# Memory attention and channel mixer in one kernel: the maxima of phi move from GpSimd to VectorE and small transfers, and the attention products go over whole tiles

## The chip, the cores and the metric

The kernel runs on one core of one Trainium2 chip. The metric is the device time of one execution in microseconds (us), as the median of several executions. TensorE multiplies matrices, VectorE, ScalarE and GpSimd work on tiles elementwise, and SyncE issues most transfers between device memory (DRAM) and the on-chip memory. Each engine, and SyncE's queue of transfers, works through its own list strictly in order.

## The reference

For each of 8 batches and 8 heads (576 positions, head size 64, 32 memory slots):

```python
a = phi - np.max(phi, axis=2, keepdims=True)          # over the positions, per memory slot
a = np.exp(a); a = a / (np.sum(a, axis=2, keepdims=True) + 1e-09)
k_m = np.einsum('bhsm,bhsd->bhmd', a, k)              # 32 keys and 32 values per head
v_m = np.einsum('bhsm,bhsd->bhmd', a, v)
scores = scale * np.matmul(q, k_m.transpose(0, 1, 3, 2))
attn = softmax(scores)                                # over the 32 slots
x = np.matmul(attn, v_m)                              # heads joined: (8, 576, 512)
h = np.maximum(x.T @ w_tok1, 0) @ w_tok2              # mixing over positions
u = x + h.T
out = u + np.maximum(u @ w_ch1, 0) @ w_ch2            # mixing over channels
```

## The kernel before, in words

A **quad** is one batch and one half of its heads (four heads); quad (4,1) is batch 4, second half. A quad's steps on TensorE are: `get_kv` (tile `kvp`, sums of keys and values over the positions), a small turn of `T` into `kb`, `scores` (tiles `sp`), `A` (tile `Ap`, the attention weights times `w_tok1`), `R` (tile `Rp`) and `u` (four tiles `u`, each one half of the channels by one half of the positions). Between `scores` and `A` lie the softmax on VectorE and ScalarE, a trip of its result through DRAM (`rows_out`, `rows_in`) that turns the layout, and a split of it into a high and a low part (`nat_high` on ScalarE, `nat_low` on GpSimd). Most products are made of such high and low parts, three products for one.

The results `u` are cut into chunks of 512 positions. The channel layers of a chunk (tiles `cp` and `acc`, 128x512 products) are the bulk of TensorE's work. The program has three parts in time. In the first, batches 0 and 1 are done between loads and conversions of the weights. In the second, the twelve quads from batch 2 on run, and the channel layers of chunks 1 and 2 fill TensorE between their steps. In the third, the remaining chunks are done in pairs by a scheme with seven products in place of eight; no quad is left there.

In the second part a planner sets the order of the work. Each step has an engine, an assumed duration in us, the steps it follows, the buffers ("rooms") it takes or uses, and a due time that serves as its rank; quad n is due `PERIOD` later than quad n-1. The planner plays the list through once and writes each engine's instructions in the order that results; on the chip nothing is reordered.

The maximum that is taken from phi before the exponential only has to be the same over the positions of one head and slot. `phi_max` (line 644, by `_red`, line 446) reduces on VectorE over the five blocks of positions within a partition, and `phi_all` (line 630) then takes the maximum over the 128 partitions with a GpSimd call. `phi_sub` (line 633, GpSimd) subtracts it, `phi_only_exp` (line 455, ScalarE) follows, and then `get_kv` can start. The planner's entries for these, as they stand in the second part:

```python
z = do(-17, "DVE", 1.35, qd.phi_max, z, take=[m], use=[phi_room])
z = do(-16, "POOL", 0.9, qd.phi_all, z, take=[r], use=[m])
z = do(-14, *PHI_SUB(qd), z, use=[phi_room, r], port=True)
e = do(-12, "ACT", 0.8, qd.phi_only_exp, z, use=[phi_room])
```

The weights of attention for `u` are kept in two tiles per quad, each with the high part of 64 rows in one half of the partitions and their low part in the other (`a_high`, `a_low`); `v_pair` (line 708) copies the high values twice to match. The tile S of the softmax has one room.

Of the kernel before, what the change touches and what calls it, by code (L numbers as in the profile page):

```python
# [20 lines left out]
P = 128  # L21
# [7 lines left out]
def kernel(  # L29
# [4 lines left out]
    phi: bass.AP,  # L34
    w_tok1: bass.AP,
# [58 lines left out]
    warm = wp.tile([P, 1], F32, tag="ps", name="warm", bufs=2)  # L94
# [5 lines left out]
    c1 = {}  # L100
# [240 lines left out]
    class Sums:  # L341
# [9 lines left out]
        def words(s):  # L351
            s.w = [sb.tile([P, 2, 256], F32, tag="al", name=f"w{j}{s.p}", bufs=2) for j in range(2)]
            for j, w in enumerate(s.w):
                h, l = (t[:, 2 * j : 2 * j + 2] for t in c1[s.p])
                nc.vector.tensor_tensor(out=w, in0=f32(h), in1=f32(l), op=ALU.add)

        def sum(s):
            t = wide(F32R, f"sums{s.p}").rearrange("p a n -> p (a n)")
            s.t = t
            s.v = v = t.rearrange("p (o x m) -> p o x m", o=4, x=2)  # L360

            def at(o):
                return f32(v[:, o, 1]).rearrange("p (a n) -> p a n", a=2)

            (w11, w21), (w12, w22) = ((w[:, :, :P], w[:, :, P:]) for w in s.w)
# [60 lines left out]
    class Quad:  # L426
# [17 lines left out]
        def _red(s, op):  # L444
            m = sb.tile([P, 4 * M], F32, tag="pr", name="pr" + s.n, bufs=3)
            nc.vector.tensor_reduce(
                out=m.rearrange("p (i m) -> p i m", i=4),
                in_=s.pt.rearrange("p i j m -> p i m j"),
                axis=AX.X,
                op=op,  # L450
            )
            return m

# [15 lines left out]
        def scales(s):  # L469
            s.ms = wp.tile([P, 6], F32, tag="ms", name="ms" + s.n, bufs=1)  # L470
            sm = wp.tile([P, 1], F32, tag="ps", name="ps" + s.n, bufs=2)
# [5 lines left out]
        def double_T(s):  # L477

            s.T = sb.tile([P, 2, D], F32, tag="pr", name="T" + s.n, bufs=3)
# [139 lines left out]
    class LateQuad(Quad):  # L619
# [4 lines left out]

        def phi_max(s):
            s.m = s._red(ALU.max)
# [17 lines left out]

        def vb_room(s):
            s.vb = side[0][:, 640:896]
            return s.vb.rearrange("p (i d) -> p i d", i=4)

        def spread_v(s):
            nc.vector.tensor_tensor(  # L650
                out=s.vb_room(),
                in0=s.kvp[:, D1 : D1 + D].unsqueeze(1).to_broadcast([P, 4, D]),
                in1=s.ms[:, 0:4].unsqueeze(2).to_broadcast([P, 4, D]),
                op=ALU.mult,
            )

        def spread_T(s):
            s.scales()
            s.double_T()
# [8 lines left out]
        def scores(s):  # L668
            s.sp = [bank([P, 512], f"sp{hf}" + s.n) for hf in range(2)]
            s.mm_s()  # L670

# [19 lines left out]
        def a_high(s, p):  # L691
            if not p:
                s.pairs = []
            s.pairs.append(sb.tile([P, S], F32R, tag="ah", name=f"a{p}" + s.n, bufs=2))
            own = slice(64 * p, 64 * p + 64)
            nc.scalar.copy(out=s.pairs[p][own], in_=s.aT[own])

        def a_low(s, p, eng):
            own, other = slice(64 * p, 64 * p + 64), slice(64 - 64 * p, P - 64 * p)
            t = s.pairs[p]  # L700
            eng.tensor_tensor(out=t[other], in0=s.aT[own], in1=f32(t[own]), op=ALU.subtract)

        def v_pair(s, p):
            if not p:
                s.vv = sb.tile([P, 2, P], F32R, tag="vb", name="vv" + s.n, bufs=1)
            own = slice(64 * p, 64 * p + 64)
            for x in range(2):
                nc.scalar.copy(
                    out=s.vv[64 * x : 64 * x + 64, p], in_=f32(s.vh[own, p * P : p * P + P])
                )  # L710
# [24 lines left out]

        def u(s, db, hf):
            s.up[db, hf] = bank([P, 512], f"u{db}{hf}" + s.n)
            s.mm_u(s.up[db, hf], db, hf)
# [215 lines left out]
    def plan(rank, ways, slow=None, slack=0.0):  # L954
# [37 lines left out]
        while left:  # L992
            times = {z: t for z in left if (t := when(z)) is not None}
            first = {}
            for z, t in times.items():
                first[z.eng] = min(first.get(z.eng, 1e9), t)
            eng = min(first, key=lambda e: (first[e], e))
# [69 lines left out]
    class EarlyQuad(Quad):  # L1067
# [19 lines left out]
        def phi_max(s):  # L1087
            s.col = wp.tile([P, 2], F32, tag="ps", name="col" + s.n, bufs=2)
# [23 lines left out]
        def keys_twice(s, keys):  # L1112
            s.T = sb.tile([P, 2, D], F32, tag="pr", name="T" + s.n, bufs=3)
# [101 lines left out]
    class FirstQuad(EarlyQuad):  # L1215
# [175 lines left out]
        def plan(s, w1, w2, taken, chunk):  # L1391
# [6 lines left out]
            T, tp = s.of("pr", 3), s.bank()  # L1398
# [52 lines left out]
    class SecondQuad(EarlyQuad):  # L1451
# [65 lines left out]
        def plan(s, w1, w2, taken, chunk, behind):  # L1517
# [5 lines left out]
            kvp, T, vb, tp, kb = s.bank(), s.of("pr", 3), s.of("vb"), s.bank(), s.of("kb")  # L1523
# [68 lines left out]
    class ThirdBatchQuad(SecondQuad):  # L1592

        for name in (
            "turn_T", "get_kb", "scores", "rows_in", "nat_low", "v_pair", "A", "R", "u", "straight", "u_high",
            "u_low", "spill", "store_u",
# [236 lines left out]
    def A_LOW(qd, p):  # L1833
        return "DVE", 0.78, lambda: qd.a_low(p, nc.vector)
# [4 lines left out]
    PERIOD, START = 13.5, 3.0  # L1839
    for n, qd in enumerate(late):  # L1840
# [5 lines left out]
        bk, kb, vh, vl, vb, T = room("at", 2), room("kb"), room("vh", 2), room("vl", 2), room("side vb"), room("pr", 3)  # L1846
        if n:
            phi_room, kv_r, q_r = room("phi", 2), room("kv"), room("qT")
            m, r = room("pr", 3), room("pr", 3)
            z = do(-25, "SP", 0.8, qd.load_phi, begin, take=[phi_room], move=0.9)  # L1850
            z = do(-17, "DVE", 1.35, qd.phi_max, z, take=[m], use=[phi_room])
            z = do(-16, "POOL", 0.9, qd.phi_all, z, take=[r], use=[m])
            way = n % 2
            z = do(-14, *PHI_SUB(qd), z, use=[phi_room, r], port=True)
            e = do(-12, "ACT", 0.8, qd.phi_only_exp, z, use=[phi_room])
# [6 lines left out]
        y = do(-8, "DVE", 0.85 if n else 0.3, qd.spread_T, z, take=[T], use=[bk])  # L1862
        v = do(-7, "DVE", 0.42, qd.spread_v, z, y, sided, take=[vb], use=[bk, side_room])
# [3 lines left out]
        vlow = do(-4, "DVE", 0.43, qd.v_low, v, take=[vl], use=[vb, vh, side_room], port=True)  # L1867
        ss, S_, mx, sm = [room("at", 2), room("at", 2)], room("S"), room("mx", 2), room("mx", 2)
        aT, vv, ah = room("aT"), room("vb"), [room("ah", 2) for p in range(2)]
        z = do(0, "PE", 1.05, qd.scores, y, lq, take=ss, use=[q_r, kb])  # L1870
        former = [z, vlow]
        ends["kv"] = [z]
        z = do(1, "DVE", 0.47, lambda qd=qd: qd.turn_S(0), z, take=[S_], use=[ss[0]])
        z = do(1.5, "DVE", 0.47, lambda qd=qd: qd.turn_S(1), z, use=[S_, ss[1]])
        z = do(2, "DVE", 0.76, qd.S_max, z, take=[mx], use=[S_])
        z = do(3, "DVE", 0.77, qd.S_sub, z, use=[S_, mx], port=True)
        z = do(3.7, "ACT", 0.7, qd.S_exp, z, use=[S_])
        z = do(4.5, "DVE", 1.25, qd.S_sum, z, take=[sm], use=[S_])
        w = z = do(5.7, "DVE", 0.77, qd.S_mul, z, use=[S_, sm], port=True)
        raw, nat = room("raw"), room("big")  # L1880
        z = do(6.5, "SP", 3.2, qd.rows_out, w, use=[S_], move=0.7)
# [554 lines left out]
```

## Time and profile before

| | us |
|---|---|
| median of 3 executions | 813.11 (811.64 to 815.18) |
| the profiled execution: its own time | 810.62 |
| the profiled execution: span from first to last instruction | 808.8 |
| TensorE busy in the span | 734.9 (91%) |
| VectorE busy | 521.8 (65%) |
| ScalarE busy | 364.5 (45%) |
| GpSimd busy | 99.1 (12%) |

TensorE, VectorE, ScalarE and GpSimd are called PE, DVE, ACT and POOL in the rows, and SyncE's queue is SP. A busy share is an average over the three parts of the program, so a table by stretches of time says more than this one: the first part ends at about 123 us, the second at about 447 us. "Granted clock" is the share of TensorE's full clock of 2.4 GHz that it was given in a stretch.

### The profile page before, as it was taken

To read this page: it belongs to the slowest core of one execution; us is meant where nothing else is said; L and a number is where in the kernel's file an instruction comes from. 1 tells how busy PE (TensorE), PEld (TensorE's weight loads), DVE (VectorE), ACT (ScalarE), POOL (GpSimd) and SP (SyncE) were. 2 spreads that over 40 slices of the span, in tenths; PEclk is the share of its full clock that TensorE was granted. 3 is DMA by queue.
4 is the path that set the end of the run, shared out by engine and by line. 5 is a ranking of instruction groups with operands and counts; after the bars stand their busy time and mean duration, and the time that the engine had idled before them with its cause. 6 is when DMAs were issued, how large, how long until landed. Compare 5 with 4: busy or idle time off the path is not lost.

```text
span 808.8 us, 11574 instructions
## 1 busy us (share of the span) xinstructions
PE 734.9 (91%) x4323; PEld 606.5 (75%) x4323; DVE 521.8 (65%) x864; ACT 364.5 (45%) x676; POOL 99.1 (12%) x93
## 2 busy tenths in 40 slices
PE   8999996596978893789699999999999999999998
PEld 7778884474866783668488877888878888788887
DVE  4999745254855573457389854697734897724883
ACT  5999651122432440334345444644434543434540
POOL 2123242111011131121104000000000000000000
PEclk9999999688998996989799999999999999999999
DMA  8964524355648385569433577915565807457602
GB/s 349 396 253 152 165 81 153 97 166 155 208 137 263 102 284 178 186 186 295 134 106 128 203 248 254 318 73 192 167 196 178 308 26 252 152 186 237 216 26 79
DMA packets 96489, 151.30 MB, mean 187 GB/s; under 512 B 39089, under 2 KB 64305, under 8 KB 92081
## 3 DMA queue, kind: packets, MB, share of 16 engines
q1 hardware_dynamic: 84736, 117.25, 42.7%
q10 hardware_dynamic: 11696, 33.31, 13.1%
q8 instruction: 34, 0.56, 0.3%
q14 instruction: 23, 0.18, 0.1%
HBM read 113.38 MB, written 37.16 MB: 186 GB/s over the span
## 4 chain that ended last, share of the span: by engine, by line
PE 68%; issue 8%; DMA 8%; DVE 6%; POOL 3%; ACT 3%; SPq 3%; ACTq 0%; POOLq 0%; DVEq 0%
PE ma L291 9%; PE mU L2222 9%; PE cp L145 9%; PE acc L168 8%; PE u L592 7%; PE mB L2222 6%; PE mc L291 5%; DMA unit<-sums 3%; PE mA L2222 3%; PE mD L2222 3%; PE Ap L576 2%; POOL phi L633 2%; DMA side<-rows 2%; DMA kv<-in_kv_dram 1%; PE kvp L461 1%
## 5 line engine op out<-in xcount | busy, mean ns | idle before, releaser
L168 PE MATMUL acc<-hh,c 128*128 128x512 f32 x288 | 104.1, 413 | 0.0
L168 PEld LDWEIGHTS acc<-hh,c 128*128 128x128 f32 x288 | 56.9, 198 | 17.4 <-issue 5.5
L168 PE MATMUL acc<-hl,c 128*128 128x512 f32 x144 | 58.4, 406 | 0.0
L455 ACT ACTIVATE phi<-phi 128x640 f32<-128x640 f32 x11 | 8.1, 737 | 103.0 <-POOL phi L633 103.0
L145 PE MATMUL cp<-uh,c1h 128*128 128x512 f32 x144 | 54.5, 419 | 0.0
L145 PE MATMUL cp<-ul,c1h 128*128 128x512 f32 x144 | 51.6, 399 | 0.0
L145 PE MATMUL cp<-uh,c1l 128*128 128x512 f32 x144 | 51.6, 399 | 0.0
L117 DVE SCALAR_TENSOR_TENSOR hl<-cp,hh 128x512 fp32r<-128x512 f32 x36 | 24.7, 686 | 32.5 <-ACT hh L114 32.3
L2208 ACT CAST rT<-hid 128x512 fp32r<-128x512 f32 x54 | 32.0, 621 | 26.8 <-PE mB L2222 15.6
L2209 DVE TENSOR_TENSOR rT<-hid,rT 128x512 fp32r<-128x512 f32 x54 | 35.7, 685 | 7.0 <-ACT rT L2208 7.0
L576 PE MATMUL Ap<-w1h,nat 128*128 128x256 f32 x126 | 26.8, 307 | 14.1 <-POOL nat L689 8.5
L592 PE MATMUL u<-a,vv 128*128 128x288 f32 x56 | 18.2, 326 | 23.3 <-ACT side L748 16.3
L2076 DVE TENSOR_TENSOR hid<-mb,hid 128x512 f32<-128x512 f32 x12 | 8.3, 692 | 47.5 <-ACT hid L2156 47.4
L592 PE MATMUL u<-w2h,Rh 128*128 128x288 f32 x112 | 35.2, 314 | 2.1 <-ACT Rh L114 2.1
L592 PE MATMUL u<-w2h,Rl 128*128 128x288 f32 x112 | 34.9, 312 | 0.2 <-DVE Rl L117 0.2
L592 PE MATMUL u<-w2l,Rh 128*128 128x288 f32 x112 | 35.0, 312 | 0.0
L145 PEld LDWEIGHTS cp<-uh,c1h 128*128 128x128 f32 x144 | 27.3, 194 | 9.4 <-issue 4.9
L114 ACT ACTIVATE hh<-cp 128x512 fp32r<-128x512 f32 x36 | 21.5, 598 | 28.2 <-PE cp L145 21.2
L748 ACT COPY side<-u 128x288 f32<-128x288 f32 (+1 forms) x44 | 17.1, 390 | 37.9 <-PE u L592 36.9
L576 PEld LDWEIGHTS Ap<-w1h,nat 128*128 128x128 f32 x126 | 21.6, 207 | 16.0 <-POOL nat L689 9.3
L689 POOL TENSOR_TENSOR nat<-side,nat 128x512 fp32r<-128x512 f32 (+1 forms) x24 | 22.0, 916 | 86.4 <-ACT nat L681 73.9
L145 PEld LDWEIGHTS cp<-uh,c1l 128*128 128x128 f32 x144 | 27.7, 193 | 6.3
(366 smaller groups left out, 1982.2 us busy)
## 6 DMA issues: line engine op xcount, KB each, us to landing
unit<-sums ACTq DMA_DIRECT2D x54, 512.0 KB, 4.8
kv<-in_kv_dram SPq DMA_DIRECT2D x12, 1300.0 KB, 5.9
rawc<-in_w_ch_dram SPq DMA_DIRECT2D x12, 1024.0 KB, 7.1
q<-in_q_dram SPq DMA_DIRECT2D x16, 576.0 KB, 4.3
sums<-sums SPq DMA_DIRECT2D x12, 512.0 KB, 5.0
u_p<-spilled SPq DMA_DIRECT2D x6, 1024.0 KB, 6.8
phi<-in_phi_dram SPq DMA_DIRECT2D x16, 320.0 KB, 6.2
unit<-sums ACTq DMA_DIRECT2D x18, 256.0 KB, 3.2
```

The source lines that it names most:

```text
L114: nc.scalar.activation(out=h, in_=ps, func=AF.Relu)
L117: nc.vector.scalar_tensor_tensor(out=l, in0=ps, scalar=0.0, in1=f32(h), op0=ALU.max, op1=ALU.subtract)
L145: nc.tensor.matmul(ps, l[:, a, w], r[:, a], start=n == 0, stop=n == len(mm) - 1)
L168: nc.tensor.matmul(ps, l_[f // 2][:, f % 2, a * P : (a + 1) * P], r[:, w], start=f == start and x == 0, stop=f == end - 1 and x == 2,)
L291: nc.tensor.matmul(ps, l, r, start=first and n == 0, stop=n == len(mm) - 1, skip_group_check=not first,)
L576: nc.tensor.matmul(ps[:, :TT], a, w, start=x == 0, stop=x == len(mm) - 1)
L592: nc.tensor.matmul(ps[:, :HALF], a, r, start=x == 0, stop=x == len(mm) - 1)
L689: eng.tensor_tensor(out=o, in0=a, in1=f32(h), op=ALU.subtract)
L748: nc.scalar.copy(out=side[0][:, o + n : o + HALF], in_=ps[:, n:HALF])
L2208: nc.scalar.copy(out=t[:, 0], in_=x)
L2209: nc.vector.tensor_tensor(out=t[:, 1], in0=x, in1=f32(t[:, 0]), op=ALU.subtract)
L2222: nc.tensor.matmul(s.banks[room][a][:, w], l_[:, a * P : a * P + P], r_, start=not (p or x) and name in ("11", "T1", "21", "T4"), stop=p = ...
```

## The change

Quads from (2,1) on get the maxima in another way. The host gives phi a second time in a layout with one head and slot in each partition (`phi_turned`, 128x576 for a quad). `load_turned` loads it, `phi_max` reduces it on VectorE to 128x1, `max_out` writes these 128 numbers to DRAM, and `max_in` reads them back to all 128 partitions. All three transfers are issued by SyncE. The GpSimd call is gone; `phi_sub` stays on GpSimd.

```diff
-        def phi_all(s):
-            s.r = sb.tile([P, 4 * M], F32, tag="pr", name="prr" + s.n, bufs=3)
-            nc.gpsimd.partition_all_reduce(s.r, s.m, P, RED.max)
+        def load_turned(s):
+            s.turned = sb.tile([P, S], F32, tag="al", name="phiT" + s.n, bufs=2)
+            nc.sync.dma_start(out=s.turned, in_=phi_turned[s.b - 2, s.Q])
...
+            s.m = wp.tile([P, 1], F32, tag="ps", name="m" + s.n, bufs=3)
+            nc.vector.tensor_reduce(out=s.m, in_=s.turned, axis=AX.X, op=ALU.max)
+
+        def max_out(s):
+            s.top = dram.tile([1, 4 * M], F32, name="top" + s.n, tag="maxima", bufs=2)
+            nc.sync.dma_start(out=s.top.rearrange("a n -> n a"), in_=s.m)
+
+        def max_in(s):
+            s.r = sb.tile([P, 4 * M], F32, tag="pr", name="prr" + s.n, bufs=2)
+            nc.sync.dma_start(out=s.r, in_=s.top.to_broadcast([P, 4 * M]))
```

The weights of attention are split into one whole high tile and one whole low tile. `v_pair` is gone; the products use 64 of the 128 rows of the array, with the two halves of the channels in turn, into two open tiles `u`:

```diff
+        def attend(s, hf):
+            w = slice(hf * HALF, (hf + 1) * HALF)
+            for db in range(2):
+                s.up[db, hf] = bank([P, 512], f"u{db}{hf}" + s.n)
+            for x, (v, a) in enumerate(((s.vh, s.ah), (s.vh, s.al), (s.vl, s.ah))):
+                for db in range(2):
+                    own, m = slice(64 * db, 64 * db + 64), slice(db * P, (db + 1) * P)
+                    nc.tensor.matmul(s.up[db, hf][:, :HALF], v[own, m], a[own, w], start=x == 0, stop=False)
```

S can lie in its own room or in one of the two rooms "al", which the sums of the channel weights (`words`) no longer use. The scaling of the keys (`spread_T`) goes to ScalarE. The planner's entries follow, with some assumed durations a little different, and the steps are due every 12.0 us a quad in place of 13.5:

```diff
-    PERIOD, START = 13.5, 3.0
+    PERIOD, START, behind = 12.0, 3.0, []
...
-            z = do(-17, "DVE", 1.35, qd.phi_max, z, take=[m], use=[phi_room])
-            z = do(-16, "POOL", 0.9, qd.phi_all, z, take=[r], use=[m])
...
+            y = do(-32, "SP", 0.5, qd.load_turned, begin, take=[turned], move=0.9)
+            y = do(-27, "DVE", 0.72, qd.phi_max, y, take=[m], use=[turned])
+            y = do(-26, "SP", 0.5, qd.max_out, y, use=[m])
...
+            y = do(-22, "SP", 0.5, qd.max_in, y, z, take=[r])
```

**The order that results.** The first part and the third are as before, engine by engine. Names end in batch, half and a buffer's number, so `prr_3_0` belongs to quad (3,0). On GpSimd, at the start of the second part, before the change (the rows named ISA are instructions that come with the call):

```order
L179 TENSOR_TENSOR o_0_1351<-uh_0_460,ul_0_461 128x512 x4
L630 ISA
L630 ISA prr_2_1_1466<-pr_2_1_1445 128x128
L633 ISA
L633 TENSOR_TENSOR phi_2_1_1388<-phi_2_1_1388,prr_2_1_1466 128x640
L630 ISA
L630 ISA prr_3_0_1546<-pr_3_0_1524 128x128
L633 ISA
L633 TENSOR_TENSOR phi_3_0_1412<-phi_3_0_1412,prr_3_0_1546 128x640
```

and with it:

```order
L180 TENSOR_TENSOR o_0_1351<-uh_0_460,ul_0_461 128x512 x4
L631 TENSOR_TENSOR phi_2_1_1411<-phi_2_1_1411,prr_2_1_1498 128x640
L631 TENSOR_TENSOR phi_3_0_1431<-phi_3_0_1431,prr_3_0_1549 128x640
L695 TENSOR_TENSOR nat_2_0_1701<-side_1422,nat_2_0_1701 128x512
L695 TENSOR_TENSOR nat_2_0_1701<-side_1422,nat_2_0_1701 64x128
```

All 33 ISA rows of the eleven calls are gone; the subtractions stand next to each other.

On SyncE's queue, the start of the second part with the change (`top` holds the maxima in DRAM, `prr` is what `max_in` reads, `out_dram` the store of chunk 0):

```order
L441 DMA q_2_1_1469<-in_q_dram 128x1152
L189 DMA out_dram<-o_0_1351 128x2048
L628 DMA prr_2_1_1498<-top_2_1_1459 128x128
L624 DMA top_3_0_1505<-m_3_0_1491 128x1
L616 DMA phiT_4_0_1507<-in_phi_turned_dram 128x576
L624 DMA top_3_1_1529<-m_3_1_1521 128x1
L616 DMA phiT_4_1_1535<-in_phi_turned_dram 128x576
L628 DMA prr_3_0_1549<-top_3_0_1505 128x128
L544 DMA rows_2_0_1557<-S_2_0_1467 32x18x32 x4
```

and further on in the same queue:

```order
L436 DMA kv_4_0_2035<-in_kv_dram 128x2600
L431 DMA phi_4_1_2047<-in_phi_dram 128x640
L628 DMA prr_4_1_2054<-top_4_1_1613 128x128
L624 DMA top_6_1_2070<-m_6_1_2060 128x1
L616 DMA phiT_7_1_2077<-in_phi_turned_dram 128x576
L624 DMA top_7_0_2093<-m_7_0_2075 128x1
```

For the first two quads the maxima go out and come back within a few transfers; further on they are written several quads ahead of their use (that of (6,1) behind the read of (4,1)).

On TensorE, the start of `u` of quad (2,0), before:

```order
L592 MATMUL u00_2_0_1838<-a0_2_0_1726,vv_2_0_1430 128x288
L592 MATMUL u00_2_0_1838<-a0_2_0_1726,vl_2_0_1436 128x288
L592 MATMUL u00_2_0_1838<-w2h_96,Rh_2_0_1800 128x288
L592 MATMUL u00_2_0_1838<-w2l_97,Rh_2_0_1800 128x288
L592 MATMUL u00_2_0_1838<-w2h_96,Rl_2_0_1810 128x288
```

and with the change:

```order
L736 MATMUL u00_2_0_1866<-ah_2_0_1567,vh_2_0_1429 128x288
L736 MATMUL u10_2_0_1867<-ah_2_0_1567,vh_2_0_1429 128x288
L736 MATMUL u00_2_0_1866<-al_2_0_1575,vh_2_0_1429 128x288
L736 MATMUL u10_2_0_1867<-al_2_0_1575,vh_2_0_1429 128x288
L736 MATMUL u00_2_0_1866<-ah_2_0_1567,vl_2_0_1437 128x288
L736 MATMUL u10_2_0_1867<-ah_2_0_1567,vl_2_0_1437 128x288
L745 MATMUL u00_2_0_1866<-w2h_96,Rh_2_0_1842 128x288
```

The attention products of two tiles alternate ahead of the mixing products of the first.

## Rows read from the trace of the kernel before

**Rows 1.** Table by stretch: each engine's busy us (instructions), granted clock, DMA share, GB/s.

```profile
20.00:123.00 103.00, 102.99 (x668) 84.77 (x668) 81.88 (x126) 82.81 (x140) 32.11 (x18) 1.00 0.58 207
123.00:447.20 324.20, 259.10 (x1861) 213.87 (x1860) 193.75 (x352) 113.40 (x258) 62.70 (x57) 0.88 0.56 174
447.20:808.80 361.60, 356.06 (x1577) 292.41 (x1575) 236.97 (x368) 157.44 (x263) 0.00 (x0) 1.00 0.54 184
```

**Rows 2.** The same table for a short stretch behind a wait.

```profile
143.80:149.00 5.20, 5.14 (x47) 4.01 (x48) 1.70 (x4) 1.18 (x3) 0.00 (x0) 0.50 0.29 86
```

**Rows 3.** Waits of PE, 123 to 447.2 us: total us, times, longest.

```profile
PE u L592 <- ACT side L748: 16.3, 2, 12.6
PE sp L501 <- ACT kb L666: 14.1, 2, 7.9
PE Ap L576 <- POOL nat L689: 8.5, 2, 5.3
PE kvp L461 <- ACT phi L455: 8.5, 1, 8.5
PE u L592 <- DVE ul L194: 6.5, 1, 6.5
PE Ap L576 <- ACT nat L681: 4.5, 1, 4.5
```

**Rows 4.** The chain that ended last, one piece: start, us, what.

```profile
299.96 2.74 PE cp L145 x12
...
305.42 2.12 PE u L592 x16
307.55 9.91 issue
317.46 1.53 POOL phi L633
...
320.09 3.83 PE u L592 x16
```

**Rows 5.** POOL in order of time: start, us, instruction [idle before, its releaser].

```profile
149.01 0.72 POOL L630 PARTITION_ALL_REDUCE prr<-pr  x1 [5.98 <-issue]
...
218.32 0.73 POOL L630 PARTITION_ALL_REDUCE prr<-pr  x1 [17.74 <-DVE ul L194]
226.84 1.78 POOL L689 TENSOR_TENSOR nat<-side,nat 128x512 fp32r<-128x512 f32 x2 [7.79 <-issue]
228.70 1.55 POOL L633 TENSOR_TENSOR phi<-phi,prr 128x640 f32<-128x640 f32 x1
```

**Rows 6.** Groups of POOL, 123 to 447.2 us: count, busy us, mean ns, idle before.

```profile
L633 POOL TENSOR_TENSOR phi<-phi,prr 128x640 f32<-128x640 f32 x11 | 16.8, 1530 | 78.1 <-issue 63.2 <-DMA phi<-in_phi_dram 7.8 <-DMA side<-rows 6.9
L630 POOL PARTITION_ALL_REDUCE prr<-pr x11 | 8.7, 794 | 88.8 <-DVE pr L446 20.0 <-PE u L592 19.1 <-DVE ul L194 17.7
```

**Rows 7.** PE in order of time in the first part, with 64-row products (64*128).

```profile
26.53 1.24 PE L1389 MATMUL u<-aT,vb 64*128 64x288 f32 x8
27.70 1.13 PE L1361 MATMUL Rp<-vb,A 128*128 128x256 f32 x4
28.67 0.64 PE L1330 MATMUL at<-ident,k 128*128 128x128 f32 x4
```

**Rows 8.** Groups of DVE and ACT, 123 to 447.2 us, that the change touches.

```profile
L701 DVE TENSOR_TENSOR a<-aT,a 64x576 fp32r<-64x576 f32 x22 | 19.4, 881 | 7.9 <-ACT a L696 7.6
...
L708 ACT CAST vv<-vh 64x128 fp32r<-64x128 f32 x48 | 14.2, 297 | 0.6
```

**Rows 9.** Transfers of the whole run: count, KB each, median us from issue to landing.

```profile
phi<-in_phi_dram SPq DMA_DIRECT2D x16, 320.0 KB, 6.2
rows<-S SPq DMA_DIRECT2D x54, 72.0 KB, 2.1
```

**Rows 10.** The last quad, (7,1): its scores on PE and its low part on POOL.

```profile
412.22 0.71 PE L501 MATMUL sp<-q,kb 64*32 64x288 f32 x16
...
430.54 2.12 POOL L689 TENSOR_TENSOR nat<-side,nat 128x512 fp32r<-128x512 f32 x2 [16.66 <-ACT nat L681]
```

More of the change, by code (lines that the diff above doesn't have):

```diff
@@ L351, in words, with at @@
         def words(s):
[L352 to L355, printed above, removed]
-        def sum(s):
[L358 to L365, printed above, removed]
+            t = s.t = wide(F32R, f"sums{s.p}").rearrange("p a n -> p (a n)")
+            s.v = t.rearrange("p (o x m) -> p o x m", o=4, x=2)
+            for j in range(2):
+                h, l = (f32(t[:, 2 * j : 2 * j + 2]).rearrange("p a (o n) -> p o a n", o=2) for t in c1[s.p])
+                to = f32(s.v[:, 2 * j : 2 * j + 2, 0]).rearrange("p o (a n) -> p o a n", a=2)
+                nc.vector.tensor_tensor(out=to, in0=h, in1=l, op=ALU.add)
+        def sum(s):
+            def at(o, x=1):
+                return f32(s.v[:, o, x])
+            w11, w21, w12, w22 = (at(o, 0) for o in range(4))
             for o, x, y, op in (
@@ L670, in scores, with S_take, turn_S @@
             s.mm_s()
+        def S_take(s, room):
+            s.S = sb.tile([P, NB, M], F32, tag=room.tag, name="S" + s.n, bufs=dict(room.tags)[room.tag])
+        def turn_S(s, hf):
+            nc.vector.transpose(
+                out=s.S.rearrange("p a m -> p (a m)")[:, hf * HALF : (hf + 1) * HALF], in_=s.sp[hf][:, :HALF]
+            )
         def rows_in(s):
@@ L689, in nat_low, with a_high, a_low @@
                 eng.tensor_tensor(out=o, in0=a, in1=f32(h), op=ALU.subtract)
[L691 to L710, printed above, removed]
+        def a_high(s):
+            s.ah = sb.tile([P, S], F32R, tag="ah", name="ah" + s.n, bufs=2)
+            nc.scalar.copy(out=s.ah, in_=s.aT)
+        def a_low(s, eng):
+            s.al = sb.tile([P, S], F32R, tag="ah", name="al" + s.n, bufs=2)
+            eng.tensor_tensor(out=s.al, in0=s.aT, in1=f32(s.ah), op=ALU.subtract)
         def A(s):
@@ L996, in plan @@
                 first[z.eng] = min(first.get(z.eng, 1e9), t)
+            if not first:
+                for z in left:
+                    print("STUCK", z.eng, z.fn and z.fn.__code__.co_firstlineno, getattr(getattr(z.fn,"__self__",None),"n",""), z.fn and z.fn.__defaults__, [(r.tags, [(q.tag, sum(u.end is None for u in q.users)) for q in taken.get(r.tags[0][0], [])][-4:]) for r in z.take])
             eng = min(first, key=lambda e: (first[e], e))
@@ L2393, in _lay @@
     c2 = moe_w_ch2[:, ch.ravel()].reshape(ff // 256, 2, P, -1).transpose(0, 2, 1, 3)
+    rows_phi = rows(phi, FLOOR)
+    turned = rows_phi.transpose(0, 1, 3, 5, 4, 2).reshape(B, 2, P, -1)
+    whole = phi.reshape(B, 4, 2, S, M).transpose(0, 2, 1, 4, 3).reshape(B, 2, P, S)
     arrays = dict(
@@ L2396, in _lay @@
         kv=ones(np.stack([rows(k, 0), rows(v, 0)], axis=3).transpose(0, 1, 2, 3, 5, 4, 6)),
-        phi=planned(rows(phi, FLOOR)),
+        phi=planned(rows_phi, turned.reshape(rows_phi.shape)),
+        phi_turned=whole[2:],
         w_tok1=words(moe_w_tok1[:n].reshape(j, P, tt).transpose(1, 0, 2)),
```

156 lines of the change are left out of this document (74 added, 82 removed).

## The prediction

> **What bounds the kernel now.** I first cut the span into its three parts [rows 1]. In the first and the third TensorE is busy for 102.99 of 103.0 us and 356.1 of 361.6 us at the full clock, so nothing but fewer products could help there. The second part, 123 to 447.2 us, is different: of its 324.2 us TensorE is busy for 259.1 and idle for 65.1, and its mean granted clock is 0.88. Busy time times clock is 259.1 x 0.88 = 228.0 us of work at the full clock. So the part consists of 228.0 us of work, 65.1 us of waiting and 31.1 us of working at a lowered clock, because the clock falls behind a long wait: in the 5.2 us that follow TensorE's wait for `kvp` it is 0.50, the lower of its two levels, 1.2 GHz [rows 2, 3]. Counting the part's products gives the same: about 543 products of 128x512 at 0.2285 us (2.74/12), 50 blocks u at 1.06 (2.12/2) [rows 4], and some 51 us for the rest.
>
> Next, the waits of TensorE in this part [rows 3]. The first six groups sum to 58.4 us. They name ScalarE, GpSimd and VectorE, but none of these is short of time (ScalarE is busy for 113.4 of 324.2 us [rows 1]). So I followed the longest, 12.6 us, back along the chain [rows 4]: TensorE's products `u` end at 307.5 and go on at 320.1, and between lies 9.9 us of "issue" in which nothing that the trace shows is waited for, then the subtraction of the maxima on GpSimd. ScalarE stands at the exponential of phi behind it and can't copy the earlier `u` tiles out.
>
> What the 9.9 us are is seen in GpSimd's own rows [rows 5]. The call is recorded as 0.73 us at 218.32, but GpSimd's next instruction starts only at 226.84, after 7.79 us of idle time with no releaser. That instruction is `nat_low`, which doesn't use the maxima; the subtraction follows it at 228.70 without a gap. So the idle time belongs to the call, not to the instruction that waits. There is also 5.98 us of it ahead of a call, at 149.01 [rows 5]. The sum fits: eleven subtractions have 63.2 us of such idle time ahead of them [rows 6], and two more pieces stood there too but are put down to a transfer. A call thus costs about 8.5 us from its start to the next instruction, and up to 6 us ahead; the planner assumed 0.9. Following each wait of TensorE in this way, ten with 60.8 us in all have a call's idle time in the chain; 4.3 us have not.
>
> **What the change removes.** All eleven calls. The 60.8 us go with them, and so does the lowered clock that follows the waits. If nothing takes their place, the second part shrinks from 324.2 to about 228 us.
>
> **The products of attention.** Eight 128-row products of 288 columns per quad become twelve of 64 rows, in pairs that use the two halves of the array. The first part has such pairs [rows 7]: eight records in 1.17 us (26.53 to 27.70), 0.146 each, against 0.97 us for four records with 128 rows and 256 columns, or 0.273 for 288. The ratio is 0.53, so a pair takes about the time of one. A quad then costs 12 x 0.1325 x 0.53 = 0.84 us in place of 8 x 0.1325 = 1.06: 12 x 0.22 = 2.6 us saved, of which I take 2.4. If they didn't run side by side, they would cost 12 x (1.59 - 1.06) = 6.4 us more; I keep that for the range.
>
> **VectorE and ScalarE.** VectorE loses one of two splits per quad (0.88 us, 10.6 in all [rows 8]), reduces 576 columns of phi in place of 640, and gives the scaling of the keys to ScalarE; ScalarE loses the four copies `v_pair` (about 1.2 us a quad) and one split. VectorE's 193.8 us in the second part become at most 183. In a part of 240 us that is 76%, below the 79% (81.88 of 103) at which the first part ran without a wait [rows 1]. TensorE's work is the cover for all of it. The second room for S and the changed sums move no more work than this.
>
> **The new transfers.** Per quad there are three more in SyncE's queue. No row shows a transfer of 4 bytes per partition. The nearest is `rows<-S` with short pieces, 2.1 us to landing; an upper bound is a load of phi behind others, 6.2 us [rows 9]. I take 2.1 for each small one where the queue is quiet, since it is of their kind. From the third quad on this is hidden: the maxima are written several quads ahead in the order, and the read back is issued right behind phi's own load, which the subtraction waits for anyway. Only the first two quads, (2,1) and (3,0), have the trip in sight. There the read stands behind the store of chunk 0, which waits for VectorE until about 134 us. With 2.1 to 6.2 us for the read, the subtraction ends at 138 to 142; the order puts 57 channel products (13 us) ahead of `get_kv`, which reaches TensorE at about 142.5. For (3,0) it is tighter, since its write lies behind the same store. I allow 4 us.
>
> **What is late next.** With no call, a quad's own way from `scores` to `A` sets the pace. For the last quad, which has no call beside it, it took 412.9 to 432.7 us, 19.8 us [rows 10]. By the order, and with the durations above, the products between the two are worth 18.7 to 26.2 us; in four quads they are worth less than 20. I take 4 us for these four. Where phi's load itself is late (6.2 us [rows 9]), a wait can stay. With the 4.3 us of before I come to about 12 us of waiting in all, at a clock close to full, since no wait is long.
>
> **The sum.** The second part becomes 228.0 - 2.4 + 12 = 237.6 us, 86.6 less. The profiled execution's own time was 810.6 (span 808.8), so 724.0. The median of the runs is 2.5 above that execution: 726.5.
>
> **Rival 1: new waits take back a third.** The planner's list has quads only about 16 to 19 us apart, and all stalls in which loads could catch up are gone. If each of eleven quads comes 2 to 3 us late, that is 22 to 33 us, and at 0.48 us of lost clock per idle us (31.1/65.1) up to 49. That replaces the 12 us and gives 736 to 764, say 750. For it speaks that the loads of keys and values wait for `get_kv` in one queue with everything else; against it that the first part, planned in the same way with VectorE at 79%, has no such waits.
>
> **Rival 2: the trip of the maxima takes the place of the call (slower).** If the write and the read with 6.2 us each, a reduction of 0.7 and two issues stood between phi's landing and the subtraction for every quad, that would be 14 us, as long as a call with both its gaps; with SyncE held up for the three further issues, some 1.5 us a quad, the time would be 813 + 16 = 829. It decides from the point where the maxima are not ready before phi has landed. The order speaks against that for nine of eleven quads.
>
> **Rival 3: the idle time is not the call's.** If the 0.7 to 0.8 us recorded were the whole price of the call (8.7 us for eleven), the gaps would be GpSimd's own and would stay, and the time would be about 811. The rows speak against it [rows 5]: two tensor operations follow each other without a gap, and only a call has them on both sides. The Trainium skill (GPSIMD Engine Reference, Engine selection) gives reductions over partitions to GpSimd and would speak against this change; by it the maxima should stay where they are. The trace here disagrees in that a call holds GpSimd for about 8.5 us. The Trainium skill (DMA: Bandwidth & Descriptors, Anatomy of one DMA) gives about 2.0 us as the fixed part of any transfer, an estimate of 4 us for the trip per quad, which would change the sum only in rival 2.
>
> **Chances.** The forecast with little waiting has 0.74; its own range goes from 714 (no wait at all: 726.5 - 12) to 738 (12 us more: twice the waits, or the products not side by side and some). Rival 1 has 0.20, rival 2 0.03, rival 3 0.03. The range that leaves out about two in ten goes from 714 to 758. A measurement of this kernel can tell about 0.5%, 4 us, from no change. Faster by more: 0.95; within: 0.02 (rival 3); slower: 0.03 (rival 2).
>
> **What would show it.** Right: no POOL gap without releaser of more than 1 us; TensorE idle for 5 to 20 us in the second part and a granted clock of 0.97 or more there; ScalarE's wait for the subtraction no longer the longest; the twelve 64-row products of a quad in about 0.9 us; the second part ending at 355 to 370 us and the third unchanged at about 361 us. Wrong: TensorE waiting for `nat` or `kvp` in most quads (rival 1), SyncE's waits led by VectorE's maxima (rival 2), or a third part that now waits for VectorE or loads which the longer second part had covered.

## The result and the profile after

The changed kernel took 785.93 us (median of 4 executions, 780.99 to 790.09). The kernel before, run beside it, took 814.14. The ratio is 0.9645, 95% interval 0.9575 to 0.9716. So it is faster, as forecast, but by 28 us where 87 were expected, and the time lies above the range given. Further ratios are to the kernel before on the same chip, with the same kind of interval.

The table by stretch, for the three parts (columns as in [rows 1]; the last product `u` ends at 424.2):

```profile
20.00:123.00 103.00, 103.00 (x669) 84.76 (x669) 83.28 (x125) 82.70 (x139) 31.44 (x18) 1.00 0.57 204
123.00:424.20 301.20, 258.75 (x1917) 204.15 (x1916) 177.51 (x321) 98.32 (x210) 53.90 (x46) 0.93 0.76 199
424.20:788.00 363.80, 355.01 (x1566) 291.60 (x1564) 234.91 (x365) 156.37 (x261) 0.00 (x0) 0.99 0.54 184
```

The first and the third part are as in [rows 1]. In the second, TensorE is idle for 42.5 us (65.1 before) and the clock is at 0.93. Cut finer, the loss lies in one stretch:

```profile
140.00:160.00 20.00, 11.36 (x85) 7.76 (x84) 8.79 (x20) 3.47 (x7) 3.06 (x2) 0.74 0.77 78
160.00:180.00 20.00, 9.60 (x65) 7.53 (x65) 7.42 (x13) 3.30 (x6) 3.28 (x3) 0.66 0.82 184
180.00:200.00 20.00, 13.48 (x89) 10.34 (x87) 9.04 (x14) 5.16 (x10) 1.56 (x1) 0.92 0.93 173
200.00:220.00 20.00, 14.88 (x116) 12.00 (x116) 10.69 (x23) 6.08 (x16) 3.52 (x4) 0.83 0.93 168
220.00:240.00 20.00, 14.28 (x72) 11.35 (x66) 8.31 (x16) 3.88 (x9) 1.53 (x1) 0.74 0.72 181
240.00:260.00 20.00, 19.55 (x192) 15.25 (x191) 11.92 (x25) 8.82 (x21) 3.25 (x3) 1.00 0.70 213
```

From 140 to 240 us TensorE works for 63.6 of 100 us; from 240 us on it is nearly full. In these 100 us VectorE is busy for 44, ScalarE for 22 and GpSimd for 13, yet the DMA engines are at 0.72 to 0.93. In two shorter windows they are counted as busy and move little (a share over 1 means that more packet time is counted than the engines had):

```profile
156.00:158.00 2.00, 1.85 (x5) 1.56 (x6) 2.00 (x5) 1.19 (x3) 0.28 (x1) 0.50 0.72 10
190.00:195.00 5.00, 3.48 (x24) 2.70 (x20) 2.25 (x4) 1.93 (x4) 0.59 (x1) 1.00 1.26 38
```

10 and 38 GB/s at shares of 0.72 and 1.26, against 174 GB/s at 0.56 in [rows 1]. Which transfers run then is seen in two views, the instructions on the maxima's DRAM buffer (durations, first and last start) and the transfers of the whole run (columns as in [rows 9]):

```profile
L624 SPq DMA_DIRECT2D top<-m x11: 319/383/1837, 129.3 to 232.4; - x11
```

```profile
phi<-in_phi_dram SPq DMA_DIRECT2D x16, 320.0 KB, 7.3
rows<-S SPq DMA_DIRECT2D x54, 72.0 KB, 3.3
phiT<-in_phi_turned_dram SPq DMA_DIRECT2D x11, 288.0 KB, 10.5
prr<-top SPq DMA_DIRECT2D x11, 64.0 KB, 7.4
top<-m SPq DMA_DIRECT2D x11, 0.5 KB, 9.9
```

All eleven writes of the maxima are issued between 129.3 and 232.4 us: the disturbed stretch. Each moves 0.5 KB, and the median time to landing is 9.9 us. The transfers beside them are late too: `rows<-S` takes 3.3 us for the 2.1 of [rows 9].

GpSimd has no call and no "issue" gap any more; its idle time before the subtraction is now put down to the read back. The first three of its instructions in order of time:

```profile
147.03 1.53 POOL L631 TENSOR_TENSOR phi<-phi,prr 128x640 f32<-128x640 f32 x1 [21.38 <-DMA prr<-top]
154.75 1.53 POOL L631 TENSOR_TENSOR phi<-phi,prr 128x640 f32<-128x640 f32 x1 [6.19 <-DMA rows<-S]
175.76 1.80 POOL L695 TENSOR_TENSOR nat<-side,nat 128x512 fp32r<-128x512 f32 x2 [19.48 <-ACT nat L1517]
```

What stopped TensorE in the second part, and VectorE from 123 to 240 us (waits: total, times, longest):

```profile
PE kvp L450 <- DMA kv<-in_kv_dram: 10.4, 1, 10.4
PE u L736 <- DVE ul L195: 8.4, 1, 8.4
PE kvp L450 <- ACT phi L444: 6.1, 1, 6.1
PE Ap L565 <- DVE ul L195: 5.7, 1, 5.7
```

```profile
DVE m L620 <- DMA phiT<-in_phi_turned_dram: 31.5, 7, 9.3
```

One load of keys and values (`kv`) comes late by itself. VectorE stands at the reduction and waits for the turned phi; `ul`, the low part of an earlier result `u`, is made on VectorE as well and is late for TensorE.

### The profile page after: what moved, and what is told of

It reads as the page before. It is cut to its first block, busy times and chain, and to the rows that moved or that the text cites. A ratio compares the mean times of both kernels' runs of the same rounds, so it can differ in the third digit from the quotient of the medians.

```text
span 788.0 us, 11573 instructions
## 1 busy us (share of the span) xinstructions
PE 733.8 (93%) x4371; PEld 596.1 (76%) x4371; DVE 505.2 (64%) x830; ACT 348.6 (44%) x627; POOL 89.7 (11%) x82
## 4 chain that ended last, share of the span: by engine, by line
PE 62%; DMA 24%; DVE 4%; SPq 4%; ACT 2%; issue 2%; POOL 1%; ACTq 0%; POOLq 0%; DVEq 0%
PE ma L292 10%; PE mU L2232 9%; PE cp L146 7%; PE acc L169 7%; PE mB L2232 6%; PE mc L292 5%; DMA kv<-in_kv_dram 5%; DMA phiT<-in_phi_turned_dram 4%; DMA unit<-sums 4%; DMA rows<-S 4%; PE mA L2232 3%; DMA side<-rows 3%; PE mD L2232 3%; PE u L745 2%; PE Ap L565 2%
## 5 line engine op out<-in xcount | busy, mean ns | idle before, releaser
L169 PEld LDWEIGHTS acc<-hh,c 128*128 128x128 f32 x288 | 55.0, 191 | 16.3 <-issue 5.2
L450 PE MATMUL kvp<-kv,phi 128*32 128x130 f32 x440 | 16.6, 302 | 16.5 <-DMA kv<-in_kv_dram 10.4
L146 PEld LDWEIGHTS cp<-ul,c1h 128*128 128x128 f32 x144 | 28.1, 195 | 4.6
L292 PE MATMUL ma<-xrest_p,unit 128*128 128x512 f32 x108 | 28.1, 396 | 3.7 <-DMA unit<-sums 3.6
L745 PE MATMUL u<-w2h,Rh 128*128 128x288 f32 x96 | 31.5, 328 | 0.0
L2089 ACT ACTIVATE hid<-hid 128x512 f32<-128x512 f32 x24 | 15.2, 632 | 36.3 <-DVE hid L2086 32.1
L169 PEld LDWEIGHTS acc<-hl,c 128*128 128x128 f32 x144 | 27.7, 192 | 4.3
L631 POOL TENSOR_TENSOR phi<-phi,prr 128x640 f32<-128x640 f32 x11 | 17.1, 1551 | 118.6 <-DMA prr<-top 112.3
```

Of the source, the lines that this page charges most:

```text
L146: nc.tensor.matmul(ps, l[:, a, w], r[:, a], start=n == 0, stop=n == len(mm) - 1)
L169: nc.tensor.matmul(ps, l_[f // 2][:, f % 2, a * P : (a + 1) * P], r[:, w], start=f == start and x == 0, stop=f == end - 1 and x == 2,)
L292: nc.tensor.matmul(ps, l, r, start=first and n == 0, stop=n == len(mm) - 1, skip_group_check=not first,)
L631: eng.tensor_tensor(out=s.pt, in0=s.pt, in1=s.r.rearrange("p (i m) -> p i m", i=4) .unsqueeze(2) .to_broadcast([P, 4, NC, M]), op=ALU.subt ...
L745: nc.tensor.matmul(s.up[db, hf][:, :HALF], a, r, start=False, stop=x == len(mm) - 1)
```

## The experiments

Theory A: the write of 128 pieces of 4 bytes occupies the DMA engines, and whatever is queued behind it is late. Rivals: B, the read back is the load; C, the eleven further loads of 288 KB are; D, SyncE's queue stands while it waits for VectorE's maxima.

**e1_four_pieces.**

```diff
+            nc.vector.transpose(out=s.mt, in_=s.m.to_broadcast([P, 32]))
...
-            nc.sync.dma_start(out=s.top.rearrange("a n -> n a"), in_=s.m)
+            nc.sync.dma_start(
+                out=s.top.rearrange("a (o n) -> (a o) n", n=32), in_=s.mt.rearrange("(o x) n -> o x n", x=32)[:, 0]
+            )
```

> The 128 maxima are turned on VectorE in 32x32 blocks and written to DRAM as four pieces of 128 bytes in place of 128 pieces of 4 bytes; the read back to all partitions, the loads of the turned phi and SyncE's wait for VectorE stay. Theory A (the 4-byte pieces of the write keep the DMA engines busy, and all transfers behind them are late): the write lands in 2 to 4 us in place of 9.9, the loads of phi, keys and values in 140 to 240 us return to their medians of before (6.2 and 5.9 us), and the time falls to 730 to 755. Theory B (the read back, which fetches the same 512 bytes 128 times, is what loads the DMA engines): 775 to 790, the read still takes 7.4 us. Theory C (eleven more loads of 288 KB, called up in a burst): 775 to 790, with phi turned still landing in 10 us. Theory D (SyncE's queue stands while it waits for VectorE's maxima): 775 to 790.

747.69 us (744.52 to 749.82), ratio 0.9184 (0.9143 to 0.9226): 38.2 us less than the changed kernel. The table by stretch of this run:

```profile
123.00:381.30 258.30, 248.24 (x1916) 196.58 (x1915) 178.44 (x332) 98.26 (x210) 55.71 (x46) 0.99 0.75 233
...
140.00:160.00 20.00, 20.00 (x182) 15.18 (x188) 16.51 (x35) 8.45 (x17) 7.34 (x5) 1.00 0.95 284
```

From 140 to 160 us the DMA engines are even busier than in the changed kernel (0.95 against 0.77) but move 284 GB/s in place of 78. The second part is shorter by 42.9 us: 32.4 of idle time and 10.5 of busy time, which come from the higher clock (0.99 in place of 0.93). The read back, the loads and SyncE's wait are all still in the program, so B, C and D are out.

**e2_turn_on_tensor.**

```diff
-            nc.sync.dma_start(out=s.top.rearrange("a n -> n a"), in_=s.m)
...
+            nc.tensor.transpose(s.mp[:, :P], s.m.to_broadcast([P, P]), ident)
...
-            nc.sync.dma_start(out=s.r, in_=s.top.to_broadcast([P, 4 * M]))
+            nc.scalar.copy(out=s.r, in_=s.mp[:, : 4 * M])
```

> No trip through DRAM: TensorE turns the 128 maxima (a 128x128 transpose of the column repeated) into PSUM, ScalarE copies them to the tile that the subtraction reads. The loads of the turned phi stay. Theory A and theory B (write or read of the maxima): both are gone, 725 to 745, unless the new product and copy bring waits of their own, up to 755. Theory D (SyncE waits for the maxima): also gone, 725 to 745. Theory C (the loads of the turned phi): 770 to 790.

746.08 us, 0.9166 (0.9129 to 0.9203). Without the trip it is not told apart from the run with four pieces (747.69): a trip written that way is hidden.

**e3_no_write** and **e4_no_read.**

```diff
-            nc.sync.dma_start(out=s.top.rearrange("a n -> n a"), in_=s.m)
+            s.top = phi_turned[s.b - 2, s.Q][:1, : 4 * M]
```

```diff
-            nc.sync.dma_start(out=s.r, in_=s.top.to_broadcast([P, 4 * M]))
+            nc.gpsimd.memset(s.r, 0.5)
```

> The write of the maxima is left out; the read back to all partitions takes its 512 bytes from a row of the turned phi in place of the maxima (another constant per head and slot is subtracted, which the division by the sum takes out again). Theory A: as with four pieces, 730 to 755. Theory B (the read): 775 to 790. Theory C: 775 to 790. Theory D (SyncE's wait for VectorE, which goes with the write): 730 to 755. So against the run with four pieces it parts A from D.

> The read back is left out: GpSimd fills the tile with a constant (0.5 is subtracted in place of the maxima; the division by the sum takes it out again), and everything else, the write with its 128 pieces of 4 bytes too, stays in the same order. Theory A: still 770 to 790, since the writes are unchanged, the transfers behind them as late as before; a few us less because the subtraction no longer waits for the read. Theory B: 730 to 750. Theory C and theory D: 770 to 790.

Without the write 749.31 us, 0.9202 (0.9169 to 0.9234); without the read 782.78 us, 0.9613 (0.956 to 0.9665). So the write is the cost, though in e4 nobody waits for what it writes.

**e5 to e8 and e11: the write put back beside the four pieces, in other shapes.** Only the `dump` line differs, and the order of all five is the same.

```diff
+            dump = dram.tile([P, 1], F32, name="dump" + s.n, tag="dump", bufs=11)
+            nc.sync.dma_start(out=dump, in_=s.turned[:, :1])
```

In e6 the tile is [P, 128] and the write goes to `dump[:, :1]`, in e11 [P, 16] and `dump[:, :1]`; e7 writes `s.turned[:, :16]` and e8 `s.turned[:, :128]` into whole tiles.

> The kernel with four pieces (747.7 us), and per quad one more transfer right behind the write of the maxima, whose result nobody reads: the first column of the turned phi, 128 pieces of 4 bytes, to 512 bytes of DRAM. It puts the suspected write back without anything that waits for its result. Theory A (such a write occupies the DMA engines themselves): 770 to 790. Rival E (the write is only late for its own reader, and the loss came through the subtraction that waits for it): 746 to 752.

> As the run before it, but the 128 pieces of 4 bytes go to addresses 512 bytes apart. Theory A1 (each piece of 4 bytes has a high price, wherever it goes): 770 to 790, as with neighbouring addresses. Theory A2 (pieces that fall into the same few hundred bytes of DRAM wait for each other): 746 to 755. Rival E: 746 to 752.

> The same added write with 128 pieces of 64 bytes, side by side (8 KB). If the price is that of pieces of 4 bytes alone: 746 to 755. If it is that of short pieces in general, or of 128 pieces, 765 to 790. The softmax rows, which go to DRAM in pieces of 128 bytes, landed in 2.1 us before the change, so I expect 746 to 755 by theory A.

> The same added write with 128 pieces of 512 bytes (64 KB). Control for one more transfer per quad in SyncE's queue: by theory A (short pieces) 746 to 753. If one more transfer of any kind, or 128 pieces of any size, were enough: 765 to 790.

> The kernel with four pieces and the added write of 128 pieces of 4 bytes, now 64 bytes apart (side by side it gave 809.9, 512 bytes apart 748.0). If pieces collide only within some 64 bytes or less: 746 to 755. If they collide within a few hundred bytes: 765 to 810, less than side by side.

| 128 pieces of | time, us | ratio (95%) |
|---|---|---|
| 4 bytes side by side (e5) | 809.88 | 0.9945 (0.9903 to 0.9988) |
| 4 bytes, 64 bytes apart (e11) | 750.13 | 0.9212 (0.917 to 0.9254) |
| 4 bytes, 512 bytes apart (e6) | 747.96 | 0.9175 (0.9139 to 0.9211) |
| 64 bytes side by side (e7) | 749.90 | 0.9213 (0.9158 to 0.9268) |
| 512 bytes side by side (e8) | 750.67 | 0.9206 (0.9171 to 0.9241) |

Neither the piece of 4 bytes nor the number of pieces is dear, but 4-byte pieces that are neighbours in DRAM: 62 us more than e1 for eleven such writes, 5.7 each. A1 falls, A2 stands, with a distance of 64 bytes already enough. Rival E is out: nothing waits for the added write. The loss is larger than expected for e5 (770 to 790). Its effect in e5, and the same stretch of e6:

```profile
140.00:160.00 20.00, 10.94 (x87) 7.90 (x86) 6.50 (x15) 3.61 (x7) 3.55 (x2) 0.74 0.87 116
```

```profile
140.00:160.00 20.00, 20.00 (x176) 15.25 (x175) 13.30 (x31) 8.71 (x17) 5.95 (x5) 1.00 0.88 269
```

The DMA shares are nearly equal, but 116 GB/s stand against 269. Where the trace of e6 has the landing of an added write, it took 3.3 us:

```profile
dump<-phiT SPq DMA_DIRECT2D x11, 0.5 KB, 3.3
```

The traces also hold each packet, one piece of a transfer on one DMA engine. The packets of 4 bytes took 9 ns (median) in e5 as in e6, at most 161 ns in e5. The packets of 2304 bytes, which are the rows of the turned phi, took 284 ns on average and up to 10.3 us in e5, against 114 ns and 1.3 us in e6; in the changed kernel it is 348 ns and up to 7.8 us, in e1 123 ns and 1.3 us. So the busy share with little moved is the time of loads that stand beside the writes; the writes' own pieces are recorded as short.

**e9_before_no_call, e10_rest_with_call, e12_no_maxima: the two halves of the change apart.**

```diff
-            nc.gpsimd.partition_all_reduce(s.r, s.m, P, RED.max)
+            nc.gpsimd.memset(s.r, 0.5)
```

That is e9. e10 is the changed kernel with `phi_max` and `phi_all` as before (due at other times than there), e12 the changed kernel with this fill and no maxima.

> The kernel before, in its own order, with the GpSimd call replaced by a fill of its result tile with 0.5 (another constant is subtracted; the division by the sum takes it out again). Nothing else is changed, so it measures what the call cost in the kernel before. By the forecast's step (60.8 us of waits and 31.1 us of lowered clock go): about 721, say 715 to 728. Theory F (the forecast's 228.0 us, busy time times mean granted clock, is too little work: much of the lowered clock lay in idle time and was counted as lost; the run with four pieces has 247.9 us of TensorE work in this part at a clock of 0.99): 738 to 758.

> The kernel after with the maxima as before (reduction of the five blocks on VectorE, GpSimd call), all other edits kept: 64-row products, two rooms for S, sums without extra tiles, steps due every 12.0 us. If the call is what costs, it is near the kernel before, 795 to 825. If the other edits brought a good part of what the run with four pieces gained (66 us): 760 to 790.

> The kernel after without any maxima: no load of the turned phi, no reduction, no write, no read; GpSimd fills the tile with 0.5. It is the floor for every way to get the maxima. If loads, reduction, write in four pieces and read are hidden: 738 to 750, near the run with four pieces (747.7). If the eleven loads of 288 KB (theory C) still cost what is left over the forecast: 720 to 735.

e9: 731.18 us, 0.8983 (0.8935 to 0.9031). e10: 818.48 us, 1.0054 (1.0019 to 1.0088). e12: 749.11 us, 0.9208 (0.9151 to 0.9265). So the call was worth 82 us in the kernel before, and the other edits gain nothing as long as the call is there. e9 fits neither expectation (715 to 728 and 738 to 758). e12 is not told apart from e1: the loads of the turned phi and the reductions are hidden, and C is out once more. But e12 is 18 us slower than e9, and the next runs look for these. The second part in e9:

```profile
123.60:367.70 244.10, 237.09 (x1860) 197.17 (x1859) 198.71 (x352) 115.34 (x258) 59.71 (x57) 1.00 0.75 231
```

**e13_full_rows** and **e14_pairs**, on top of e1.

```diff
-                    nc.tensor.matmul(s.up[db, hf][:, :HALF], v[own, m], a[own, w], start=x == 0, stop=False)
+                    nc.tensor.matmul(s.up[db, hf][:, :HALF], v[:, m], a[:, w], start=x == 0, stop=False)
```

```diff
-            for x, (v, a) in enumerate(((s.vh, s.ah), (s.vh, s.al), (s.vl, s.ah))):
...
+                for x, v in enumerate((s.vv[:, db], s.vl[:, db * P : (db + 1) * P])):
+                    nc.tensor.matmul(s.up[db, hf][:, :HALF], v, s.pairs[db][:, w], start=x == 0, stop=False)
```

> The kernel with four pieces (747.7 us), its twelve attention products per quad taken over all 128 rows in place of 64 (the values of the other half of the channels are zero, so the result is the same). In its trace a block of six 64-row products takes 0.80 us with the slower steps on the way in and out, 1.61 per quad; twelve 128-row products would take 12 x 0.1325 = 1.59. Theory G (the change between 64 and 128 rows eats what running in pairs saves): 745 to 750, no difference. By the forecast's step (0.84 us per quad for 64 rows): 9 us slower, 756.

> The kernel with four pieces, the attention products and their splits as before the change: eight 128-row products per quad, two tiles of high and low halves, copies of the values on ScalarE. Theory G (64 rows cost 1.61 us per quad, eight products 1.06): about 6.6 us faster, 739 to 744, if ScalarE's and VectorE's extra copies are hidden. By the forecast's step (64 rows save 2.4 us): 749 to 753. If the other edits' loss of 18 us is all in the attention part, with its waits for two open tiles u: 730 to 738.

e13: 748.16 us, 0.919 (0.9144 to 0.9237), no difference to e1. e14: 744.52 us, 0.9167 (0.9102 to 0.9232), 3 us less than e1 but within its interval, so not settled by the time alone. The work is: taken in steps of 2 us over the whole span, TensorE's busy time times its granted clock sums to 721.1 us in e1, 722.2 in e13 and 711.7 in e14 (712.5 both in the kernel before and in e9). So eight full products spare 9 us of work against the twelve. The profiled execution of e14, its slowest, loses more than that again, in idle time (26.3 us, 22.6 in e1) and at a lowered clock (12.8 us, 1.7 in e1). TensorE in order of time shows where the 64-row products lose. First e1, with 64 rows:

```profile
240.59 0.39 PE L146 MATMUL cp<-uh,c1l 128*128 128x512 f32 x1
240.91 0.40 PE L740 MATMUL u<-ah,vh 64*128 64x288 f32 x2
241.15 0.29 PE L740 MATMUL u<-al,vh 64*128 64x288 f32 x2
241.28 0.29 PE L740 MATMUL u<-ah,vl 64*128 64x288 f32 x2
241.51 0.40 PE L749 MATMUL u<-w2h,Rh 128*128 128x288 f32 x1
241.74 0.29 PE L749 MATMUL u<-w2l,Rh 128*128 128x288 f32 x1
```

and e13, with 128:

```profile
241.90 0.39 PE L146 MATMUL cp<-uh,c1l 128*128 128x512 f32 x1
242.13 0.42 PE L740 MATMUL u<-ah,vh 128*128 128x288 f32 x2
242.39 0.43 PE L740 MATMUL u<-al,vh 128*128 128x288 f32 x2
242.65 0.42 PE L740 MATMUL u<-ah,vl 128*128 128x288 f32 x2
242.91 0.29 PE L749 MATMUL u<-w2h,Rh 128*128 128x288 f32 x1
243.04 0.30 PE L749 MATMUL u<-w2l,Rh 128*128 128x288 f32 x1
```

From the last channel product to the second mixing product it is 1.15 us with 64 rows and 1.14 with 128. Two 64-row products do run side by side (the two of a record take 0.40 and 0.29 us together, no longer than one full product, and the pairs follow each other after 0.24 and 0.13 us). But the step into them is 0.32 us in place of 0.23, the first pair takes 0.24 in place of 0.13, and the way out takes 0.23 and 0.23 in place of 0.13 and 0.13. That eats the gain. The Trainium skill (TensorEngine Tiling (Array Packing), Tiling Modes) says that a change of the tiling mode drains TensorE. These rows fit that: the steps in and out cost some 0.4 us more than between full products.

**e15_period, e16_maxima_alone, e18_replanned, e19_one_room: the order.**

```diff
-    PERIOD, START, behind = 12.0, 3.0, []
+    PERIOD, START, behind = 13.5, 3.0, []
```

```diff
-            z = do(-16, "POOL", 0.9, qd.phi_all, z, take=[r], use=[m])
+            z = do(-16, "POOL", 0.2, qd.phi_all, z, take=[r], use=[m])
```

```diff
-        S_ = Room(("S", 1), ("al", 2))
+        S_ = Room(("S", 1))
```

These are e15 and e19 (on e1), and between them e18 (on e9). e16 is the kernel before with the maxima as in e1 and the attention products, rooms for S, due times and scaling as before; there the turned phi shares its two rooms "al" with the sums of the channel weights.

> The kernel with four pieces, steps due every 13.5 us a quad in place of 12.0. Theory H (the closer due times crowd the early quads and starve TensorE of other work later): 735 to 743. If the order does not matter: 745 to 750.

> The kernel before with only the way of the maxima changed: turned phi, reduction on VectorE, write in four pieces of 128 bytes, read back; attention products, rooms for S, due times and scaling as before. Without the call and without any maxima that kernel took 731.2. If loads, reduction, write and read are hidden there too, as they are in the changed kernel: 730 to 738, and the other edits are what costs the rest. If this way needs the other edits (second room for S, closer due times): 742 to 755.

> The kernel before without the call (731.2 us), with one number of the planner's list changed: the step that now fills a tile is assumed at 0.2 us in place of 0.9. All work is the same, only the order of the second part comes out differently. Theory I (which order the list happens to give moves the time by ten us and more, with nothing else changed): more than 5 us off 731.2, 737 to 760. If orders that are planned with right durations are about as good: 728 to 736.

> The kernel with four pieces (747.7 us), with one room for S in place of S or one of the two rooms that the turned phi uses. If the one room is what made the maxima alone slow in the kernel before (768.8 us, VectorE there waited 17 us for the rows of S to be written): 757 to 775. If the loss there lay in the order only: 744 to 752.

e15: 752.08 us, 0.9236 (0.919 to 0.9282): not faster than e1, so theory H falls, though it is 2 us above the other expectation. e16: 768.77 us, 0.9437 (0.9383 to 0.949), where I had expected 730 to 738; dearer than either expectation. e18: 748.29 us, 0.9161 (0.9079 to 0.9243): one assumed duration, nothing else, costs 17 us against e9, or 14 by the two ratios. TensorE's work is the same there (713.2 us, summed as above, 712.5 in e9); idle time grows by 9.0 us and 8.7 are lost at a lowered clock. So theory I holds: which order the list happens to give moves the time by about as much as e9 and e12 differ. e19: 756.60 us, 0.9269 (0.9199 to 0.9339), 9 us more than e1 and between its two expectations. One room also makes another order, so these 9 us are not shown to be the room's own price. In e16 the largest piece of TensorE's idle time from 120 to 420 us (8.8 of 30.6) lies at the end of the second part, where the channel products run out:

```profile
380.00:400.00 20.00, 11.21 (x55) 9.94 (x54) 9.81 (x16) 7.07 (x15) 2.17 (x2) 0.66 0.46 154
```

Whether the order, the one room for S or the shared rooms "al" make e16 slow was not tried on it.

The best versions that take real maxima are e1, e2, e13 and e14, at 744.5 to 748.2 us: faster than both kernels, and not told apart from each other.

## Why the prediction was wrong

**What bounds the kernel: right in kind.** The call was the cause: without it (e9) the kernel before falls from 813 to 731 us. Rival 3 (the gaps are GpSimd's own) is refuted by e9. Rival 2 came about in part: GpSimd's subtraction does wait for the read back, but where it doesn't (e4) the time is only 3 us less, no more than the scatter of the runs. Of what was to be seen, the GpSimd gaps are gone and the third part is unchanged; the clock of the second (0.93), its end (424 us) and the 64-row products (1.58 us a quad) were not as told. (The chance of "faster by more" should have been 0.94, the sum of 0.74 and 0.20.)

**The step that failed: "The new transfers".** I took the write of the maxima for a transfer like `rows<-S`, 2.1 us where the queue is quiet, hidden from the third quad on, and allowed 4 us for the start. It took 9.9 us to landing, and the read back 7.4. Above all it was priced by its own reader only, while its price is what it does to the transfers beside and behind it: 38 us (785.9 against 747.7), 3.5 per write. The bound of 6.2 us was no bound either, because the row it came from has long pieces (2560 bytes). The read back and the loads cost nothing to be seen (e1 against e12), as forecast. Rival 1 foresaw lost time of this size and a wait for `kvp`, but put it down to quads that are too close; in e1 the quads are due as close, and the loss is gone with the write.

**The term "228.0 us of work" was 9 us too small.** Busy time times the mean granted clock counts the clock of the idle time too. In the 9.4 us of the longest wait, before the change, TensorE is never busy and the clock is at 0.61 all the same:

```profile
307.60:317.00 9.40, 0.00 (x0) 0.00 (x0) 1.97 (x5) 0.00 (x0) 0.00 (x0) 0.61 0.61 205
```

Taken in steps of 2 us, the same busy time times the clock of each step sums to 236.9 us. Without the call, with the same products at a clock of 1.00, TensorE is busy for 237.1 us (the row of e9). So only some 22 of the 31.1 us put down to the lowered clock (259.1 - 237.1) were there to be won. The count of products seemed to confirm 228, but its "some 51 us for the rest" has no row of its own; with 237.1 us the same count leaves 60 for the rest.

**The 64-row products** were to save 2.4 us and cost about 6: 12 quads x 2 blocks x 0.79 us (1.15 - 0.23 - 0.13) = 19.0 us, against 12 x 1.06 = 12.7. The ratio of 0.53 was read inside a row of eight such products [rows 7], which has no way in and out, and against products of another kind. The work that e14 spares (9 us) is of this size. The bound I kept for the range (6.4 us if they did not run side by side) was the right size by luck, since they do run side by side.

**"What is late next" had the right size, by luck.** With the write mended, e1 has 10.1 us of idle time in the second part (258.3 - 248.2); I had 12. But I had put the waits between `scores` and `A`, and no wait of e1 stands at `A`: 7.3 of the 10.1 us stand at `u`. Its second part is still 20.7 us longer than the 237.6 forecast: 9.1 of work left out, 8.7 of 64-row products (2.4 not saved and 6.3 lost), less 1.9 of idle time; the other 4.8 hold a few more channel products in this part and the clock of 0.99, and are not traced further.

Added up on the whole kernel: 726.5 + 38.2 (write) + 9.1 (work) + 8.7 (64 rows, from rows) = 782.5, where 785.9 was measured. That the sum comes so near is in part luck, since the order alone moves the time by up to 17 us (e18). In the profiled executions of e9 and e12 (spans 729.1 and 746.2) the difference is 7.0 us of work, 5.4 of idle time and 4.7 lost at a lowered clock, summed as above. The first fits the 64-row products; whether the order or another edit makes the rest stays open, since each edit also makes another order. Why the writes cost 3.5 us each where the kernel waits for them and 5.7 where it does not (e5) stays open too.

## What to carry to other kernels

Price a small transfer by what it does to the queue, not by its bytes and its own reader: 512 bytes cost more than 288 KB here, and after a turn in 32x32 blocks on VectorE its cost was no longer to be seen (747.7 us, and 749.3 without a write). The work of a stretch at the full clock is read from a run without the waits, or from busy time times clock in short steps, not from busy time times the mean clock of a stretch with waits. Where a list sets the order, change one number that should not matter and run it before an edit is credited with 10 us, or charged with them.

## What was not expected of the hardware

Writes of 128 pieces of 4 bytes to neighbouring DRAM addresses held up the other transfers (10 GB/s at a busy share of 0.72 in a window of 2 us); the same pieces 64 bytes apart, or pieces of 64 bytes side by side, did not. The Trainium skill (DMA: Bandwidth & Descriptors, Specifications) says that below 512 B the engines read, modify and write. By that one would expect all of e5, e6, e7 and e11 to be slow; only e5 is (809.9 against 748.0 to 750.1). So short pieces alone are not dear here, but 4-byte pieces that lie closer than 64 bytes. How near is near enough was not tried, and why such writes hold up loads is not shown.
